# One core of Trainium2, attention with a gated MLP: the groups of values' products moved behind the last dense products of a block of keys

## The chip, the cores and the metric

The kernel runs on one core of a Trainium2 chip. The metric is the device time of one execution in microseconds (us). Six engines matter here: TensorE (PE in the profile, with its weight loads as PEld), VectorE (DVE), ScalarE (ACT), GpSimd (POOL), and SyncE (SP), which issues the DMAs in this kernel. Each engine works through its own list of instructions in order, and semaphores hold an instruction until what it needs is done. Products are summed in PSUM, which has eight banks of 128 x 512 numbers of 32 bits.

## What is computed

S = 2048 positions of width 512, one batch. `x` goes through an attention of 32 heads of width 16 that looks back over 255 positions and itself, and through an MLP of width 1792 with GELU; a gate of one number per position mixes the two. Cut to what matters:

```python
qkv = (x @ wqkv).reshape(B, S, 3, H, Dh)...      # H = 32, Dh = 16
scores = einsum("bhqd,bhkd->bhqk", q, k) * Dh ** -0.5
mask = (i - j >= 0) & (i - j < 256)
p = softmax(where(mask, scores, -1e9))
a = einsum("bhqk,bhkd->bhqd", p, v)... @ wo
b = gelu(x @ w1 + b1) @ w2 + b2
g = sigmoid((x * gate_w).sum(-1, keepdims=True))
out = g * a + (1 - g) * b
```

## The kernel before, in words

**Dense products.** Every dense product of 512 columns is made of three (lines 108 to 110), since each operand is split into a leading part and a rest. `dense()` (L913) is one long generator of these triples: the projections of four pieces of 512 positions, then eight turns of the MLP (`mlp`, L767), then the output projection (`final`, L857). A turn takes one piece and one half of the 1792 hidden columns. First comes its stage "u", seven hidden tiles of four triples each, with a GELU of six steps on ScalarE and VectorE behind each (`gelu`, L715); then its stage "y", 28 triples into four outputs. `fill(ns)` (L926) takes triples from the generator until a time has been filled up.

**Attention in units.** The heads are worked in 8 groups of four (g), the keys in 16 blocks of 128 (kb): 128 units u. The main loop (L943) goes over u; the maxima run LEAD = 12 units ahead of the rest. A unit has four parts i = 0 to 3. Each part has one score product for a row maximum (`att_max`, L519, tile `sm`, maximum taken by VectorE at L524) and one transposed score product (`att_exp`, L564, tile `st`, exponential by ScalarE at L586 into a tile `pt`), and then a quarter of a unit's dense work. The parts go in pairs, except in stage "u", where each goes alone: with m, s and f for the three, a unit is "m s m s f f m s m s f f" outside stage "u" and "m s f m s f m s f m s f" in it. A quarter is shorter than a triple, so now and then an f brings nothing. POOL cuts the edges of the exponentials to the window (L580).

**The values' products.** `att_pvs(u)` (L592) does nothing unless u is the last of four blocks, which are one piece of 512 positions. Then it makes one group: up to six blocks of keys, four heads, two halves, as small products that use 64 x 32 tiles of the array (L608), 2,880 in 32 groups. They sum into two tiles, `pv_sm` and `pv_st`. ScalarE copies one out (L629) and VectorE adds the other (L632); the sum is stored to DRAM (L636), and later divided (`att_norm`, L642).

**PSUM.** The dense products have two banks (tag d), the score products for the maxima three (tag sm), those for the exponentials three (tag st). A group takes one bank of tag sm and one of tag st until L629 and L632 have read them.

**What sets the order.** The order on each engine is the order in which the program writes instructions. A virtual clock places all that is not on TensorE: `after(ns, fn)` puts a step in a list of due times, and `tick(ns)`, called behind each product with its nominal length, writes the steps that have come due. `need(...)` writes steps early if something written now depends on them. `att_pvs` ticks for six pairs of blocks.

**Where the group stood.** In the unit u behind the four blocks (u divisible by 4), part i = PVAT = 2, behind its `st` product, for u up to 116 (lines 961 and 962). For the later u the group came at the unit's end (lines 969 and 970), and the last one inside the output projection (L983). Behind line 970 the unit's end also has the loads that SP issues for the next piece: keys (`load_ks`, L472) and values (`att_load_v`, L505, into the half of `vbuf` that the group just made was the last to read).

Of the kernel before, what the change touches and what calls it, by code (L numbers as in the profile page):

```python
# [32 lines left out]
def gated_mix(ctx: ExitStack, tc: tile.TileContext, x, wqkv, wo, w1, b1, w2, b2, gate_w, out):  # L33
# [81 lines left out]
    def after(ns, fn, *args):  # L115
        now[1] += 1
        heapq.heappush(todo, (now[0] + ns, now[1], fn, args))
# [7 lines left out]
    def tick(ns):  # L125
        now[0] += ns
        while todo and todo[0][0] <= now[0]:
            step_todo()

    def need(*keys):  # L130
        for key in keys:
            while key not in done:
                step_todo()
# [326 lines left out]
    def load_ks(g_, c):  # L460


        ready(c, g_, 1)
        n = 2 * NB
        put_pairs([f32(ks[64 * s + 4:64 * s + 52, slot(g_, c)]) for s in range(2)], SK[c], g_)
# [16 lines left out]
    def load_kd(g_, c):  # L482
        for t in range(max(c - 1, 0), c + 1):
            ready(t, g_, 1)
            k0 = 0 if t == c else T - W
            at = W if t == c else 0
            src = heads(SK[t], g_)[:, :, :, :, k0:].rearrange("s d u a c -> (s d u) a c")
            nc.sync.dma_start(f32(kd[0:96, slot(g_, c), :, at:at + T - k0]), src)

    def load_qd(g_, c):  # L490
        ready(c, g_, 0)
        put_pairs([f32(qd[48 * s:48 * s + 48, slot(g_, c)]) for s in range(2)], SQ[c], g_)

    def load_qs(g_, c):
        ready(c, g_, 0)
        need(("v", NT - 2, NB - 1))
        for s in range(2):
            v = f32(qs[64 * s + 4:64 * s + 52, :, c * T:(c + 1) * T])
            nc.sync.dma_start(v, part(SQ[c], g_, s).rearrange("r (a c) -> r a c", a=2))

    def att_load_v(g_, c):
        need(*[("v", c, b) for b in range(NB)])
        vt = vbuf[:, c % 2]
        dst = vt[:, 0:NB * 68].rearrange("p (j c) -> p j c", c=34)
        nc.sync.dma_start(dst, SV[c].rearrange("p j s c -> p (j s) c")[:, :, 34 * g_:34 * g_ + 34])  # L505
        vts[g_, c] = vt

    def att_max(g_, b, i):

        if b % RB == 0 and (g_, b // RB) not in Ms:  # L510
            Ms[g_, b // RB] = sb.tile([128, 2 * RB, 2], F32, tag="M", bufs=2, name=f"M{g_}_{b}")
        M = Ms[g_, b // RB]
        hb, pr = divmod(i, 2)
        c, n = b // NB, slot(g_, b // NB)
        j = 2 * (b % NB) + hb
        w = min(64 * (2 * b + hb + 1), W + 64)
        k1 = 64 * (j + 1) + W
        p = ps.tile([128, 320], F32, tag="sm", bufs=3, name=f"sm{g_}_{b}_{i}")
        nc.tensor.matmul(p[:, :w], qd[0:96, n, pr, 128 * j:128 * (j + 1)], kd[0:96, n, pr, k1 - w:k1],  # L519
                         start=True, stop=True)  # L520
        junk = cs.tile([128, 320], BF16, tag="jm", bufs=1, name=f"jm{g_}_{b}_{i}")

        def red():
            nc.vector.tensor_tensor_reduce(junk[:, :w], p[:, :w], mask[:, 320 - w:320], 1.0, -3e38,  # L524
                                           ALU.add, ALU.max, M[:, 2 * (b % RB) + hb, pr:pr + 1])
            done.add(("max", g_, b, i))
        tick(w / 2.4 + 13)
        after(100, red)
# [63 lines left out]
    def att_pvs(u):  # L592

        g_, kb = divmod(u, NKB)
        c, k = divmod(kb, NB)
        if k < NB - 1:
            return
        blocks = list(range(max(kb - 5, 0), kb + 1))
        pairs = list(zip(blocks, reversed(blocks) if c else blocks))
        n = g_ * NT + c - 1  # L600
        if n >= 0:
            need(("nd", *divmod(n, NT)))
        pv = [ps.tile([128, T], F32, tag=tag, bufs=3, name=f"pv{g_}_{c}_{tag}") for tag in ("st", "sm")]

        def mm(b, i, hf, q, e, rhs, start, stop):
            r = 64 * (1 ^ hf ^ i % 2)
            v = 68 * (b % NB) + 17 * (i % 2 * 2 + i // 2)
            nc.tensor.matmul(pv[r // 64][32 * i:32 * i + 32, q - c * T:e - c * T],  # L608
                             vts[g_, b // NB][r:r + 64, v:v + 32], rhs(r),
                             start=start, stop=stop, skip_group_check=True, tile_position=(r, 32 * i))  # L610
        if c == 0:
            for i in range(4):
                mm(0, i, 1, 0, 64, lambda r: nil[r:r + 64].broadcast_to([64, 64]), True, False)
        for j, pair in enumerate(pairs):
            for hf, b in enumerate(pair):
                need(("pt", g_, b, hf))
            ends = []
            for i in range(4):
                for hf, b in enumerate(pair):
                    k0 = b * 128 + hf * 64  # L620
                    q, e = max(k0, c * T), min(k0 + W + 64, S, (c + 1) * T)
                    mm(b, i, hf, q, e, lambda r: pts[g_, b][r:r + 64, hf, i // 2, q - k0:e - k0],
                       j == 0 and not (c == 0 and hf == 1), j == len(pairs) - 1)
                    ends.append(e - q)
            tick(max(ends) * 1.6 + 40)
        nd = sb.tile([128, T], F32, tag="tmp", bufs=3, name=f"nd{g_}_{c}")

        def half():
            nc.scalar.activation(nd, pv[0], AF.Copy)  # L629

        def ev():
            nc.vector.tensor_add(nd, nd, pv[1])  # L632
            after(HOLD if g_ * NT + c < NQ - 4 else 800, store)

        def store():
            nc.sync.dma_start(ND[c][g_ // 2][g_ % 2], nd)  # L636
            done.add(("nd", g_, c))
            if g_ % 2 == 1:
                after(NORM if g_ * NT + c < NQ - 4 else 3500, att_norm, c, g_ // 2)
        after(100, half), after(700, ev)  # L640
# [285 lines left out]
    def fill(ns):  # L926

        owed[0] += ns
        while owed[0] > 0:
            c = next(run)  # L930
            if c is None:
                owed[0] = -1e9
            else:
                owed[0] -= c
                tick(c)

    NU = NG * NKB
# [5 lines left out]
    for u in range(-LEAD, NU):  # L943
        m = u + LEAD
        gm, bm = divmod(m, NKB)
        step = STEP if u >= 0 else STEP0
        for i in range(4):
            if i == 1 and m % NB == 0 and NB <= m < NU - NB:
                load_kd(*divmod(m // NB + 1, NT)), load_qd(*divmod(m // NB + 1, NT))
            if i % 2 == 0:  # L950
                pair = (i, i + 1) if stage[0] != "u" else (i,)
            elif len(pair) == 2:
                continue
            else:
                pair = (i,)
            for op, i in [(op, k) for k in pair for op in ORDER[:3]] + [("f", k) for k in pair]:
                if op == "s" and u >= 0:
                    att_exp(u // NKB, u % NKB, i)
                if op == "m" and m < NU:
                    att_max(gm, bm, i ^ XOR)  # L960
                if op == "p" and i == PVAT and 1 <= u <= NU - LEAD:
                    att_pvs(u - 1)
                if op == "f":
                    fill(step / 4)
        if m < NU and bm % RB == RB - 1:
            after(900, att_rows, gm, bm // RB)
        if m % NB == QAT % NB and QAT <= m < QAT + NKB:
            load_qs(0, (m - QAT) // NB)
        if u > NU - LEAD:
            att_pvs(u - 1)  # L970
        if u % NB == 0 and NB <= u < NU - NB:
            load_ks(*divmod(u // NB + 1, NT))
        if u % NB == 2 and NB < u < NU - 3 * NB:
            load_qs(*divmod(u // NB + 3, NT))
        if u % NB == 0 and u >= 0:
            att_load_v(*divmod(u // NB, NT))
        if u - NU + NKB == YAT:
            for k in range(6):
                after(1500 + YGAP * k, load_y, *divmod(k, 2))
# [17 lines left out]
LEAD = 12  # L997
# [18 lines left out]
MXAT = 5500.0  # L1016
AHEAD = 9e3
STEP0 = 2750.0
PVAT = 2
HELD = 2  # L1020
YAT = 5
YGAP = 2500
# [21 lines left out]
```

## Time and profile before

| what | value |
|---|---|
| median of 3 runs | 750.57 us (749.57 to 752.2) |
| the profiled execution | 749.65 us |
| its span, first to last instruction | 747.9 us |
| granted TensorE clock | 1.00 |
| instructions | 17,961 |
| bytes read from and written to HBM | 108.53 MB, 62.39 MB |

Times below are in us from the start of the span unless a row says ns. In a row of a group the columns are: line, engine, operation, output<-inputs, shape, count | busy us, mean ns | idle time of the engine before it, with what ended it. In a row of the timeline: start, duration, engine, line, operation, shape, count, and in brackets the idle time ahead of it with what ended it. A TensorE row's duration is longer than the distance to the next row's start, since products overlap; the distance between two starts is what a product costs. A row of waits has the sum, the number of cases and the longest. A row of a window has, behind the stretch and its length, the busy time and count of each engine, then the granted clock, the share of the DMA engines and GB/s.

### The profile page before, as it was taken

How to read it: one execution, taken by the hardware profiler on the slowest of the kernel's cores; microseconds unless marked ns; L12 is line 12 of the kernel's file. 1: busy time of each engine (PE TensorE's matmuls, PEld its weight loads, DVE VectorE, ACT ScalarE, POOL GpSimd, SP SyncE). 2: the span in 40 equal slices, each digit the busy share in tenths (PEclk: the TensorE clock that was granted, in tenths of full speed). 3: DMA queues.
4: the chain of work that ended last, by engine and by line, in shares of the span. 5: the costliest groups of instructions: out<-in, count | busy, mean ns of one | idle time of the engine just before them, and what ended most of it. 6: DMA issues, size and time to landing. Idle time of an engine off the chain costs nothing.

```text
span 747.9 us, 17961 instructions
## 1 busy us (share of the span) xinstructions
PE 732.7 (98%) x6129; PEld 604.4 (81%) x6129; DVE 520.1 (70%) x1567; ACT 421.5 (56%) x972; POOL 372.3 (50%) x846
## 2 busy tenths in 40 slices
PE   8999999998999999999999999999999999999998
PEld 7888888876788888888887877888888888867786
DVE  4532325799768867986798689768867986784552
ACT  4434532358537845864695478438745863794550
POOL 4200000339756865876577568747765875630000
PEclk9999999999999999999999999999999999999999
DMA  9889798998895687899575979996799799468572
GB/s 326 319 272 404 261 391 273 291 293 182 270 259 134 162 243 205 175 222 271 146 179 149 242 211 234 249 237 152 178 256 235 194 224 270 136 181 226 191 252 111
DMA packets 179260, 172.12 MB, mean 230 GB/s; under 512 B 56673, under 2 KB 122977, under 8 KB 179169
## 3 DMA queue, kind: packets, MB, share of 16 engines
q1 hardware_dynamic: 179168, 170.97, 81.4%
q8 instruction: 49, 0.80, 0.5%
q14 instruction: 43, 0.34, 0.1%
HBM read 108.53 MB, written 62.39 MB: 229 GB/s over the span
## 4 chain that ended last, share of the span: by engine, by line
PE 85%; DVE 5%; ACT 3%; issue 3%; DMA 2%; SPq 1%; POOL 1%; DVEq 0%; ACTq 0%
PE sm L519 9%; PE st L564 8%; PE pv_sm L608 7%; PE y L108 7%; PE y L109 6%; PE y L110 6%; PE u L108 5%; PE u L109 5%; PE u L110 5%; PE qk L110 4%; PE qk L108 4%; PE qk L109 4%; PE a L108 2%; DVE jm L524 2%; PE v L108 2%
## 5 line engine op out<-in xcount | busy, mean ns | idle before, releaser
L524 DVE CUSTOM_DVE_ANT_0 jm<-sm,mask 128x320 bf16<-128x320 f32 (+4 forms) x512 | 238.1, 465 | 95.3 <-PE sm L519 61.1
L580 POOL TENSOR_SCALAR_AFFINE_SELECT pt<-pt 64x256 f32<-64x256 f32 (+1 forms) x538 | 227.7, 443 | 108.5 <-ACT pt L586 98.1
L586 ACT ACTIVATE pt<-st 128x320 f32<-128x320 f32 (+4 forms) x512 | 199.6, 424 | 139.1 <-PE st L564 136.0
L519 PE MATMUL sm<-kd,qd 96*128 96x320 f32 (+4 forms) x512 | 153.9, 312 | 6.3 <-DVE M L524 5.5
L564 PE MATMUL st<-qs,ks 128*128 128x320 f32 (+4 forms) x512 | 153.9, 309 | 1.9 <-ACT pt L586 1.9
L546 POOL CAST qs<-tt 4x256 fp32r<-4x256 f32 x256 | 124.6, 487 | 53.3 <-DVE tt L539 42.7
L519 PEld LDWEIGHTS sm<-kd,qd 96*128 96x128 f32 x512 | 96.3, 188 | 33.2 <-DVE M L524 13.7
L564 PEld LDWEIGHTS st<-qs,ks 128*128 128x128 f32 x512 | 97.1, 190 | 18.8 <-ACT pt L586 3.2
L108 PE MATMUL y<-w,h 128*128 128x512 f32 x224 | 88.5, 395 | 0.0
L109 PE MATMUL y<-w,h 128*128 128x512 f32 x224 | 87.9, 393 | 0.0
L110 PE MATMUL y<-w,h 128*128 128x512 f32 x224 | 87.9, 392 | 0.0
L108 PE MATMUL u<-mx,w 128*128 128x512 f32 x196 | 80.0, 408 | 0.0
L109 PE MATMUL u<-mx,w 128*128 128x512 f32 x196 | 77.4, 395 | 0.0
L110 PE MATMUL u<-mx,w 128*128 128x512 f32 x196 | 77.1, 393 | 0.0
L608 PE MATMUL pv_sm<-pt,vbuf 64*32 64x320 f32 (+4 forms) x1408 | 73.6, 346 | 0.2
L608 PE MATMUL pv_st<-pt,vbuf 64*32 64x320 f32 (+4 forms) x1408 | 73.3, 346 | 0.0
L608 PEld LDWEIGHTS pv_sm<-pt,vbuf 64*32 64x32 f32 x1408 | 50.2, 106 | 20.2 <-issue 2.4
L325 DVE TENSOR_TENSOR qke<-qk,qke 128x512 fp32r<-128x512 f32 x32 | 22.0, 688 | 46.9 <-ACT qke L322 33.2
L322 ACT ACTIVATE qke<-qk 128x512 fp32r<-128x512 f32 x32 | 19.1, 597 | 56.2 <-PE qk L110 32.5
L110 PEld LDWEIGHTS y<-w,h 128*128 128x128 f32 x224 | 42.0, 188 | 9.8
L338 POOL MEMSET vx<- 128x32 f32 x16 | 2.4, 156 | 89.0 <-DMA SQ<-qke 44.5
L608 PEld LDWEIGHTS pv_st<-pt,vbuf 64*32 64x32 f32 x1408 | 46.1, 106 | 0.0
(148 smaller groups left out, 1332.7 us busy)
## 6 DMA issues: line engine op xcount, KB each, us to landing
kd<-SK SPq DMA_DIRECT2D x32, 384.0 KB
qs<-SQ SPq DMA_DIRECT2D x64, 192.0 KB
mx<-XT SPq DMA_DIRECT2D x24, 512.0 KB
SQ<-qke SPq DMA_DIRECT2D x16, 512.0 KB
SK<-qke SPq DMA_DIRECT2D x16, 512.0 KB
ND<-nd SPq DMA_DIRECT2D x32, 256.0 KB
raw_w<-in_B_w_dram SPq DMA_DIRECT2D x28, 256.0 KB
ks<-SK SPq DMA_DIRECT2D x32, 192.0 KB
```

Source lines behind the costliest of these rows:

```text
L108: nc.tensor.matmul(p, lh, rh, start=first, stop=False)
L109: nc.tensor.matmul(p, lh, rl, start=False, stop=False)
L110: nc.tensor.matmul(p, ll, rh, start=False, stop=last)
L322: nc.scalar.activation(e[:, h], p, AF.Copy)
L325: nc.vector.tensor_sub(e[:, 1 - h], p, f32(e[:, h]))
L519: nc.tensor.matmul(p[:, :w], qd[0:96, n, pr, 128 * j:128 * (j + 1)], kd[0:96, n, pr, k1 - w:k1], start=True, stop=True)
L524: nc.vector.tensor_tensor_reduce(junk[:, :w], p[:, :w], mask[:, 320 - w:320], 1.0, -3e38, ALU.add, ALU.max, M[:, 2 * (b % RB) + hb, pr:pr ...
L546: nc.gpsimd.tensor_copy(dst, src.unsqueeze(1).broadcast_to([4, 2, RB, 32]))
L564: nc.tensor.matmul(p[:, :w], ks[:, slot(g_, kb // NB), pr, at:at + 128], qs[:, pr, k0:k0 + w], start=True, stop=True)
L580: nc.gpsimd.affine_select(out=v, in_=v, pattern=[[0, v.shape[1]], [1 - 2 * e, 64]], compare_op=ALU.is_ge, fill=0.0, base=-e, channel_multi ...
L586: nc.scalar.activation(pt[:, hf, pr, :w], p[:, :w], AF.Exp, scale=SCALE)
L608: nc.tensor.matmul(pv[r // 64][32 * i:32 * i + 32, q - c * T:e - c * T], vts[g_, b // NB][r:r + 64, v:v + 32], rhs(r), start=start, stop=s ...
```

## The change

The branch that wrote the group at part PVAT goes, with the constant, and the condition at the unit's end is widened, so that every group but the last is written there.

```diff
                 if op == "m" and m < NU:
                     att_max(gm, bm, i ^ XOR)
-                if op == "p" and i == PVAT and 1 <= u <= NU - LEAD:
-                    att_pvs(u - 1)
                 if op == "f":
                     fill(step / 4)
         if m < NU and bm % RB == RB - 1:
             after(900, att_rows, gm, bm // RB)
         if m % NB == QAT % NB and QAT <= m < QAT + NKB:
             load_qs(0, (m - QAT) // NB)
-        if u > NU - LEAD:
+        if u >= 1:
             att_pvs(u - 1)
         if u % NB == 0 and NB <= u < NU - NB:
             load_ks(*divmod(u // NB + 1, NT))
...
-PVAT = 2
```

NU is 128, LEAD 12, NB 4. What moves on the engines is shown at one group, that of the second piece of the third four heads (about 332 us into the span), in a stage "y". On TensorE, where the group begins, before (names: `sm_4_3` is block 4, part 3 of a maximum's product; `y_01` an output of the MLP; `pv_1` the group):

```order
L519 MATMUL sm_4_3_4555<-kd,qd 128x320
L564 MATMUL st_8_2_4558<-qs,ks 128x320
L608 MATMUL pv_1_sm<-pt_2_4129,vbuf 32x64
L608 MATMUL pv_1_st<-pt_7_4473,vbuf 32x64
L608 MATMUL pv_1_st<-pt_2_4129,vbuf 32x64
```

and now:

```order
L519 MATMUL sm_4_3_4555<-kd,qd 128x320
L564 MATMUL st_8_2_4558<-qs,ks 128x320
L519 MATMUL sm_4_2_4561<-kd,qd 128x320
L564 MATMUL st_8_3_4565<-qs,ks 128x320
L108 MATMUL y_00_4404<-w_6_2109,h_6_4402 128x512
L109 MATMUL y_00_4404<-w_6_2109,h_6_4402 128x512
L110 MATMUL y_00_4404<-w_6_2109,h_6_4402 128x512
L108 MATMUL y_01_4511<-w_3_1884,h_3_4142 128x512
L109 MATMUL y_01_4511<-w_3_1884,h_3_4142 128x512
L110 MATMUL y_01_4511<-w_3_1884,h_3_4142 128x512
L608 MATMUL pv_1_sm<-pt_2_4127,vbuf 32x64
L608 MATMUL pv_1_st<-pt_7_4473,vbuf 32x64
```

The unit's last pair of score products and two triples have moved ahead of the group. On TensorE, where the same group ends, before:

```order
L608 MATMUL pv_1_sm<-pt_2_4129,vbuf 32x128
L519 MATMUL sm_4_2_4617<-kd,qd 128x320
L564 MATMUL st_8_3_4622<-qs,ks 128x320
L108 MATMUL y_00_4404<-w_6_2119,h_6_4402 128x512
L109 MATMUL y_00_4404<-w_6_2119,h_6_4402 128x512
```

and now:

```order
L608 MATMUL pv_1_sm<-pt_2_4127,vbuf 32x128
L519 MATMUL sm_5_1_4643<-kd,qd 128x320
L564 MATMUL st_9_0_4648<-qs,ks 128x320
L519 MATMUL sm_5_0_4652<-kd,qd 128x320
L564 MATMUL st_9_1_4656<-qs,ks 128x320
L108 MATMUL y_01_4511<-w_4_1931,h_4_4213 128x512
L109 MATMUL y_01_4511<-w_4_1931,h_4_4213 128x512
```

Two pairs of the next block follow the group, where one pair and dense products did. On VectorE, around the addition that empties the group's second buffer (L632), before (`jm_4_2` is a maximum, the row behind it reads the result out, L812 ends an output of the MLP):

```order
L524 ISA jm_4_2_4619,M_4_4528<-sm_4_2_4617,mask 128x320
L524 ISA M_4_4528 128x1
L632 TENSOR_TENSOR nd_1_4616<-nd_1_4616,pv_1_sm 128x512
L812 SCALAR_TENSOR_TENSOR yo_00_4638<-y_00_4404,ya_00_1658 128x512
L524 ISA jm_5_1_4647,M_4_4528<-sm_5_1_4645,mask 128x320
```

and now:

```order
L524 ISA jm_4_2_4563,M_4_4524<-sm_4_2_4561,mask 128x320
L524 ISA M_4_4524 128x1
L812 SCALAR_TENSOR_TENSOR yo_00_4580<-y_00_4404,ya_00_1658 128x512
L524 ISA jm_5_1_4645,M_4_4524<-sm_5_1_4643,mask 128x320
L524 ISA M_4_4524 128x1
L524 ISA jm_5_0_4654,M_4_4524<-sm_5_0_4652,mask 128x320
L524 ISA M_4_4524 128x1
L632 TENSOR_TENSOR nd_1_4638<-nd_1_4638,pv_1_sm 128x512
L524 ISA jm_5_3_4671,M_4_4524<-sm_5_3_4669,mask 128x320
```

Two maxima of the next block stand ahead of the addition, where one maximum of the old block stood.

## The prediction

> **What bounds the kernel now.** The page comes first: its line of busy time, its chain of waits, and its costliest groups.
>
> ```profile
> span 747.9 us, 17961 instructions
> PE 732.7 (98%) x6129; PEld 604.4 (81%) x6129; DVE 520.1 (70%) x1567; ACT 421.5 (56%) x972; POOL 372.3 (50%) x846
> PE 85%; DVE 5%; ACT 3%; issue 3%; DMA 2%; SPq 1%; POOL 1%; DVEq 0%; ACTq 0%
> PE sm L519 9%; PE st L564 8%; PE pv_sm L608 7%; PE y L108 7%; PE y L109 6%; PE y L110 6%; PE u L108 5%; PE u L109 5%; PE u L110 5%; PE qk L110 4%; PE qk L108 4%; PE qk L109 4%; PE a L108 2%; DVE jm L524 2%; PE v L108 2%
> ```
>
> TensorE is the engine that sets the end: 85% of the chain, and all but 15.2 us (747.9 - 732.7) of the span. Its work is the same before and after. So the change can pay or cost in two ways only: what TensorE loses where one kind of product follows another, and what it waits for at the places that move. The view of waits on TensorE tells how much waiting there is at all.
>
> ```profile
> PE sm L519 <- DVE M L524: 5.5, 11, 1.0
> PE pv_st L608 <- ACT pt L586: 0.7, 1, 0.7
> PEld sm L519 <- DVE M L524: 13.7, 27, 1.2
> PEld st L564 <- ACT pt L586: 3.2, 6, 1.5
> PEld pv_st L608 <- ACT pt L586: 1.4, 2, 0.9
> ```
>
> The largest sum is a score product whose buffer VectorE has not read yet (L524): 13.7 us in 27 cases, counted on the weight loads, which see a wait longer than the products do. Values' products (L608) wait twice in 32 groups. So the trace holds some 18 us of such waiting (13.7 + 3.2 + 1.4), and little of it at the groups themselves.
>
> **What moves.** A group comes once in four blocks of keys, 32 in all; the branch that goes took blocks 1 to 116, so 29 of them move and three (blocks 120, 124 and the last) stay. Here is one as it is, from the timeline of TensorE: the last scores ahead, the group's first product, its last, and what follows (columns: start, duration, what).
>
> ```profile
> 332.16 0.31 PE L519 MATMUL sm<-kd,qd 96*128 96x320 f32 x1
> 332.31 0.31 PE L564 MATMUL st<-qs,ks 128*128 128x320 f32 x1
> 332.55 0.24 PE L608 MATMUL pv_sm<-pt,vbuf 64*32 64x64 f32 x1
> ...
> 334.75 0.27 PE L608 MATMUL pv_sm<-pt,vbuf 64*32 64x128 f32 x1
> 334.95 0.41 PE L519 MATMUL sm<-kd,qd 96*128 96x320 f32 x1
> 335.21 0.31 PE L564 MATMUL st<-qs,ks 128*128 128x320 f32 x1
> 335.36 0.39 PE L108 MATMUL y<-w,h 128*128 128x512 f32 x1
> 335.59 0.40 PE L109 MATMUL y<-w,h 128*128 128x512 f32 x1
> ```
>
> The group takes 2.40 us (332.55 to 334.95). What moves ahead of it is one pair of scores (0.15 + 0.15 us from start to start) and two dense triples (six products 0.23 apart, 1.39 us). So it starts about 1.7 us later; in a hidden stage ("u") it is one triple, one pair, one triple, which is the same 1.7 us. No instruction is added or taken away on TensorE.
>
> **Edge of the group, in.** After a score product the group starts 0.24 us later where 0.15 is usual (332.31 to 332.55): 0.09 lost. After a dense product, which is what the change makes of all 29, there are rows too, since the last groups already stand so.
>
> ```profile
> 686.54 0.40 PE L109 MATMUL y<-w,h 128*128 128x512 f32 x1
> 686.77 0.40 PE L110 MATMUL y<-w,h 128*128 128x512 f32 x1
> 687.10 0.24 PE L608 MATMUL pv_sm<-pt,vbuf 64*32 64x64 f32 x1
> ```
>
> 0.33 us where 0.23 is usual: 0.10 lost. The difference is 0.01 us, 29 times: 0 to +0.3 us, and I take +0.1.
>
> **Edge of the group, out.** To a score product: 0.20 (334.75 to 334.95), and then 0.26 instead of 0.15 (334.95 to 335.21). To a dense one, in a stage "u":
>
> ```profile
> 183.37 0.27 PE L608 MATMUL pv_st<-pt,vbuf 64*32 64x128 f32 x1
> 183.57 0.50 PE L108 MATMUL u<-xt,w 128*128 128x512 f32 x1
> 183.90 0.39 PE L109 MATMUL u<-xt,w 128*128 128x512 f32 x1
> ```
>
> Again 0.20, and then 0.33 instead of 0.23. Afterwards all 29 are followed by scores; by these rows that is worth 0.01 us each either way: -0.3 to +0.3 us, taken as 0. A page of the Trainium skill, "TensorEngine Tiling (Array Packing)", section "Key Properties", says that changing the tiling mode, not just the tile, drains TensorE. By that rule, the trace agrees: each change of shape costs something, about 0.1 us in and, by the rows above, some 0.2 us out. The rule alone would leave the sum as it is, since the count of changes, two per group, stays.
>
> **Waits at the group's entry.** Two of the 29 show one.
>
> ```profile
> 382.57 0.36 PE L564 MATMUL st<-qs,ks 128*128 128x320 f32 x1
> 383.60 0.30 PE L608 MATMUL pv_st<-nil,vbuf 64*32 64x64 f32 x2 [0.66 <-ACT pt L586]
> ...
> 654.89 0.30 PE L564 MATMUL st<-qs,ks 128*128 128x320 f32 x1
> 655.32 0.24 PE L608 MATMUL pv_st<-nil,vbuf 64*32 64x64 f32 x1
> ```
>
> 1.03 and 0.43 us where 0.24 is usual: 0.8 + 0.2 = 1.0 us of waiting for an exponential to leave its buffer. With at least one triple (0.70 us) between, most of it goes at the group. But the next score pair now stands there ahead of the group, and needs a buffer of the same three; in the first case ScalarE is a full us behind, so that pair can wait in the group's place. Bounds -1.0 to 0; I take -0.5, the middle, since one of the two ends is reached only if ScalarE catches up.
>
> **What stands behind the group.** Six score buffers are shared by products and group (three of a kind, the group holds one of each until its sums are read). Now both score pairs of the next block follow at once, or one pair and a triple, where one pair and dense work followed. VectorE has two maxima to take before it adds the group's halves, and till then the maxima's products turn in two buffers. From the same group, the row of ScalarE's half first and then VectorE:
>
> ```profile
> 335.08 0.60 ACT L629 ACTIVATE nd<-pv_st 128x512 f32<-128x512 f32 x1 [1.99 <-PE pv_sm L608]
> ...
> 335.41 0.49 DVE L524 CUSTOM_DVE_ANT_0 jm<-sm,mask 128x320 bf16<-128x320 f32 x1 [1.28 <-PE sm L519]
> 335.82 0.68 DVE L632 TENSOR_TENSOR nd<-nd,pv_sm 128x512 f32<-128x512 f32 x1
> 336.42 0.68 DVE L812 SCALAR_TENSOR_TENSOR yo<-y,ya 128x512 f32<-128x512 f32 x1
> 337.10 0.49 DVE L524 CUSTOM_DVE_ANT_0 jm<-sm,mask 128x320 bf16<-128x320 f32 x1
> ...
> 337.74 0.49 DVE L524 CUSTOM_DVE_ANT_0 jm<-sm,mask 128x320 bf16<-128x320 f32 x1
> ```
>
> Two maxima in a row start 0.64 us apart (337.10, 337.74). Put behind the same group, with its first score at 334.95: first maximum 335.41 to 335.90, second 336.05 to 336.54, then the add to about 337.2. The third score product comes at 334.95 + 0.26 + 3 x 0.15 + 1.39 = 337.05 and needs the first maximum: 1.1 us to spare. The fourth comes at 337.35 and needs the second: 0.8 us. In the groups where one triple stands there instead of two, 0.7 us less: 0.4 and 0.1 us. So nothing waits where VectorE has these alone. Where another addition (0.68) gets between, the fourth product can wait up to 0.6 us in those groups, five by the order. In the hidden stages VectorE is nearly full:
>
> ```profile
> 235.00:250.00 15.00, 15.00 (x103) 12.88 (x98) 13.92 (x45) 13.54 (x30) 12.22 (x26) 1.00 0.51 125
> ```
>
> 13.92 of 15 us, and still TensorE loses nothing there (15.00 of 15): a third score follows two triples and two pairs behind the group (about 2.0 us) and has room for one operation of 0.7 us ahead of its maximum (0.46 + 0.7 + 0.49 = 1.65), though not for two (2.35: 0.35 us of wait). By the order 13 groups are followed by stage "u". Bounds: 0, and 5 x 0.6 + 13 x 0.35 = +7.5 us if every one is hit. I take +0.4, near the lower end, because that row shows the engine as full as it gets and no wait. The fourth pair of the group's own block has lost its cover too, and follows the third as it does in the other three blocks of four. There 27 of 512 score products waited, 0.51 us each (13.7 / 27): 29 x 27 / 512 x 0.51 = 0.8 us. Bounds 0 and +0.8; I take +0.2, because the rest before the last group is only 1.7 us longer ago than it was.
>
> **The load of values.** It overwrites a half of vbuf that the group still reads, so SP's queue stops at it until the group's end. One such place, on SP, with the group's last product ahead of it:
>
> ```profile
> 368.51 0.27 PE L608 MATMUL pv_sm<-pt,vbuf 64*32 64x128 f32 x1
> ...
> 366.83 0.51 SPq L477 DMA_DIRECT2D ks<-SK  x1
> 368.91 0.54 SPq L505 DMA_DIRECT2D vbuf<-SV  x1
> 371.94 0.40 SPq L170 DMA_DIRECT2D raw_w<-in_B_w_dram  x1
> ```
> ```profile
> SPq L505 <- PE pv_sm L608: 6.6, 4, 2.1
> L178 ACT ACTIVATE w<-raw_w 128x512 fp32r<-128x512 f32 x28 | 17.7, 633 | 0.5 <-DMA raw_w<-in_B_w_dram 0.4
> ```
>
> Between 367.3 and 368.9 the queue stood still; now it stands 1.7 us longer wherever it gets there first. Behind the load wait stores of quotients and sums and, while weights come in, a raw_w load; their readers are ScalarE's copy (L178), then VectorE's subtraction. ScalarE waited for such a load for 0.4 us in the whole run, so there is little margin to see and no loss yet. In the place shown the queue is idle for 2.5 us after the load, which swallows 1.7. Bounds 0 and, with the three groups in the fourth turn losing all of it, +5; I take +0.2, near zero by that idle row.
>
> **The sum** is made against the profiled execution, 749.65 us (span 747.9 and 1.75 around it): +0.1 + 0 - 0.5 + 0.4 + 0.2 + 0.2 = +0.4, so 750.05. The median of the three runs shown is 750.57, 0.92 above that execution, so the forecast is 750.57 + 0.4 = **751.0 us**: no change. Changes below 0.3% (2.25 us here) cannot be told from none; the three runs themselves spread over 2.6 us.
>
> **Rivals.** *Faster:* scores right behind a group find VectorE with nothing left over, and the 13.7 us that weight loads of scores wait for L524 fall mostly in the block after and the block before a group. For it: the group gives VectorE over 1.2 us of rest (the 1.28 us ahead of 335.41). Against: that rest exists before too, only 1.7 us earlier. If a quarter of the waits goes: -3.4 and the -0.5 above, 750.57 - 3.9 = 746.7.
>
> *Slower, SP's queue:* the load of values holds raw_w in the fourth turn and the x loads at the turns' ends; ScalarE stops at L178 with exponentials behind it, and the scores wait for those. It decides once a load lands later than its copy stands in ScalarE's order, that is from about 0.4 us less margin than the trace shows. Two of three groups losing 1.7 us each: 750.57 + 3.4 = 754.0. Against: the 2.5 us of idle queue behind the load.
>
> *Slower, VectorE behind the group:* the two maxima ahead of the add, with an addition of the gelu between, in half the cases of the bound above: 7.5 / 2 = +3.8, so 754.3. Against: the full stretch at 235 us that loses nothing.
>
> *Slower, edges:* if a drain behind a 512-wide product were as much longer as the product (0.23 against 0.15), each of 29 entries would pay 0.08: +2.3, so 752.9. Against it is the row at 687.10, a measured 0.10. The rule on draining in the Trainium skill, "TensorEngine Tiling (Array Packing)", section "Key Properties", gives no length; a length that goes with the product would be this rival.
>
> *It does not do what it says:* the order of instructions shows 29 groups moved and all dense products ahead of them, so this one has no chance of its own.
>
> **How the numbers follow.** No change 0.54; faster 0.14; slower by SP 0.15, by VectorE 0.14, by the edges 0.03. That is faster 0.14, same 0.54, slower 0.32. The likeliest case alone spans 748.3 to 752.8 (0.3% to either side of the median). The range takes in most of both sides: 747.0 to 755.0, which leaves out most of the fastest case and the far end of the slow ones, some 2 in 10.
>
> **What would show it.** In the changed profile: products L608 still 0.33 us behind a dense start and scores 0.20 behind the group (edges right); no wait at the entries near 383 and 655 us (that term right), or a wait of a score pair there instead; VectorE's add (L632) ending some 0.6 us later behind each group, with no longer sum of sm waiting for M (that cover right, otherwise the third rival); the vbuf load issued right at the group's end in more of its 32 cases, with ScalarE's wait for raw_w still under 1 us (otherwise the second). The prediction is wrong if the waits of scores for VectorE, 13.7 us on the weight loads now, differ by more than about 3 us, or if TensorE's busy time differs while its instructions don't.

## The result, and the profile after

| | median | lowest to highest, runs |
|---|---|---|
| before | 750.74 us | 749.57 to 752.2, 6 |
| after | 755.42 us | 753.45 to 757.23, 6 |

The ratio is 1.0061, with a 95% interval of 1.0041 to 1.0082. The change makes the kernel slower by 4.7 us, where none was forecast, and the time lies above the range.

The page of the profiled execution of after (755.5 us), its lines of busy time and of the chain by engine:

```profile
span 753.8 us, 17980 instructions
PE 735.9 (98%) x6129; PEld 602.7 (80%) x6129; DVE 518.7 (69%) x1567; ACT 420.8 (56%) x972; POOL 371.7 (49%) x846
PE 85%; DVE 5%; DMA 3%; issue 3%; ACT 2%; SPq 1%; POOL 0%; DVEq 0%; ACTq 0%; POOLq 0%
```

TensorE makes the same 6,129 products and is busy 3.2 us longer. The span is 5.9 us longer; the view of waits shows what is added beside busy time:

```profile
PE sm L519 <- DVE M L524: 5.5, 9, 1.2
PEld sm L519 <- DVE M L524: 13.6, 28, 1.5
PE st L564 <- ACT nd L629: 2.6, 1, 2.6
PE st L564 <- DMA ks<-SK: 0.9, 1, 0.9
```

Scores wait for VectorE as before (13.6 us on the weight loads, 13.7 before). Two lines are new, each one single wait, and neither stands at a group that the change moved. In the timeline of TensorE:

```profile
683.04 0.39 PE L110 MATMUL y<-w,h 128*128 128x512 f32 x1
684.36 0.53 PE L564 MATMUL st<-qs,ks 128*128 128x320 f32 x2 [0.93 <-DMA ks<-SK]
...
691.07 0.40 PE L110 MATMUL y<-w,h 128*128 128x512 f32 x1
694.07 0.96 PE L564 MATMUL st<-qs,ks 128*128 128x320 f32 x2 [2.60 <-ACT nd L629]
694.83 0.63 PE L108 MATMUL y<-w,h 128*128 128x512 f32 x1
695.26 0.63 PE L109 MATMUL y<-w,h 128*128 128x512 f32 x1
```

Three losses follow one another: 1.1 us at 683 us (684.36 - 683.04 - 0.23), 2.8 at 691 (694.07 - 691.07 - 0.23), and then dense products stand 0.43 us apart instead of 0.23. That last one is the granted clock, in the windows of after:

```profile
690.00:695.00 5.00, 2.40 (x10) 1.74 (x9) 0.95 (x2) 1.51 (x4) 0.00 (x0) 0.84 0.38 121
695.00:700.00 5.00, 5.00 (x15) 3.94 (x14) 2.23 (x5) 1.69 (x5) 0.00 (x0) 0.50 0.70 220
```

The clock was 0.50 from 693.4 to 700.3 us. Setting the same dense product of both traces side by side, after is 1.08 us *ahead* at 681 us, 0.10 behind at 686, and 5.85 behind from 701 us to the end. So up to 681 us the 29 moved groups have cost TensorE nothing, and the next 20 us take 6.9: 1.1 and 2.8 of stops, and about 3.0 of half clock. No moved group lies within those 20 us; the last one, written at unit 116 (piece 0 of the last four heads), ended at 658.1, only 0.8 us later than before, since by then TensorE was 0.9 ahead.

What hangs on that group is the division of the last heads (`att_norm`), which is a chain: sums stored (ND, L636), denominators loaded (den, L646), inverted on VectorE (L650), stored (RD, L653), numerators and inverses loaded (num, rb, L658), multiplied (L662), stored (OT, L665), and loaded for the output projection (ot, L703). On VectorE, before and then after:

```profile
668.09 0.42 DVE L574 TENSOR_TENSOR pt<-pt,cut 128x256 f32<-128x256 f32 x1
668.43 0.34 DVE L650 RECIPROCAL den<-den 128x32 f32<-128x32 f32 x1
668.69 0.63 DVE L737 TENSOR_TENSOR h<-x1h,h 128x512 fp32r<-128x512 f32 x1
```

```profile
667.57 0.69 DVE L737 TENSOR_TENSOR h<-x1h,h 128x512 fp32r<-128x512 f32 x1
668.17 0.42 DVE L574 TENSOR_TENSOR pt<-pt,cut 128x256 f32<-128x256 f32 x1
669.53 0.69 DVE L731 SCALAR_TENSOR_TENSOR x1h<-sqh,x1h 128x512 f32<-128x512 f32 x1 [0.94 <-ACT sqh L728]
670.83 0.43 DVE L574 TENSOR_TENSOR pt<-pt,cut 128x256 f32<-128x256 f32 x1 [0.61 <-ACT pt L586]
671.17 0.68 DVE L725 SCALAR_TENSOR_TENSOR sqh<-sqh,x1h 128x512 f32<-128x512 f32 x1
671.78 0.34 DVE L650 RECIPROCAL den<-den 128x32 f32<-128x32 f32 x1
```

The steps of the division are due so many ns behind the group's store. With the group later, the reciprocal is written five rows later in VectorE's list, behind two rows that wait for ScalarE: 3.35 us later, though the engine itself is 1.1 us ahead. On SP, before and then after (start, duration of the issue, what):

```profile
660.05 0.34 SPq L636 DMA_DIRECT2D ND<-nd  x1
...
668.80 0.34 SPq L653 DMA_DIRECT2D RD<-den  x1
...
672.32 0.41 SPq L480 DMA_DIRECT2D ks<-SK  x1
...
677.08 0.34 SPq L636 DMA_DIRECT2D ND<-nd  x1
...
681.49 0.61 SPq L646 DMA_DIRECT2D den<-ND  x1
682.22 0.37 SPq L665 DMA_DIRECT2D OT<-num  x1
682.64 1.40 SPq L703 DMA_DIRECT2D ot<-OT  x3
...
684.55 0.43 SPq L703 DMA_DIRECT2D ot<-OT  x1
```

```profile
661.51 0.34 SPq L636 DMA_DIRECT2D ND<-nd  x1
...
672.15 0.34 SPq L653 DMA_DIRECT2D RD<-den  x1
...
674.85 0.42 SPq L480 DMA_DIRECT2D ks<-SK  x1
...
677.77 3.88 SPq L636 DMA_DIRECT2D ND<-nd  x1
...
685.11 0.61 SPq L646 DMA_DIRECT2D den<-ND  x1
685.76 1.41 SPq L703 DMA_DIRECT2D ot<-OT  x3
...
688.03 0.37 SPq L665 DMA_DIRECT2D OT<-num  x1
...
693.33 0.32 SPq L703 DMA_DIRECT2D ot<-OT  x1
```

The lateness grows from step to step: 1.5 us at the group's own ND, 3.35 at RD. SP stands at RD until 672.15, so nine transfers (RD to vbuf) are issued in a crowd. The keys (ks) in it go out 2.5 us later than before; a load of keys is what the stop at 683 us waits for. The next group's ND takes 3.88 us to issue, and its den comes 3.6 us later. And the store OT, which stood ahead of the three ot loads, now stands behind them: it is issued 5.8 us later. The fourth ot load waits for it to land and goes out 5.3 us after it, and holds SP's list meanwhile (before, it went out 2.3 us after OT, right behind the ya load, so it hardly waited). The buffer of `num` is what `nd` of piece 2's group needs next, which is the stop at 691 us; on ScalarE, after:

```profile
693.42 0.60 ACT L629 ACTIVATE nd<-pv_st 128x512 f32<-128x512 f32 x1 [6.19 <-DMA OT<-num]
```

### The profile page after: what moved, and what is told of

It reads as the page before. It is cut to its first block, busy times and chain, and to the rows that moved or that the text cites. A ratio compares the mean times of both kernels' runs of the same rounds, so it can differ in the third digit from the quotient of the medians.

```text
span 753.8 us, 17980 instructions
## 1 busy us (share of the span) xinstructions
PE 735.9 (98%) x6129; PEld 602.7 (80%) x6129; DVE 518.7 (69%) x1567; ACT 420.8 (56%) x972; POOL 371.7 (49%) x846
## 4 chain that ended last, share of the span: by engine, by line
PE 85%; DVE 5%; DMA 3%; issue 3%; ACT 2%; SPq 1%; POOL 0%; DVEq 0%; ACTq 0%; POOLq 0%
PE sm L519 10%; PE st L564 8%; PE pv_sm L608 7%; PE y L108 6%; PE y L109 6%; PE y L110 6%; PE u L108 6%; PE u L109 6%; PE u L110 5%; PE qk L110 4%; PE qk L108 4%; PE qk L109 4%; PE a L108 2%; PE v L108 2%; PE v L110 2%
## 5 line engine op out<-in xcount | busy, mean ns | idle before, releaser
L524 DVE CUSTOM_DVE_ANT_0 jm<-sm,mask 128x320 bf16<-128x320 f32 (+4 forms) x512 | 237.9, 465 | 103.1 <-PE sm L519 65.5
L586 ACT ACTIVATE pt<-st 128x320 f32<-128x320 f32 (+4 forms) x512 | 197.5, 424 | 125.0 <-PE st L564 121.2
L519 PEld LDWEIGHTS sm<-kd,qd 96*128 96x128 f32 x512 | 96.4, 188 | 34.7 <-DVE M L524 13.6
L108 PE MATMUL y<-w,h 128*128 128x512 f32 x224 | 89.5, 399 | 0.0
L109 PE MATMUL y<-w,h 128*128 128x512 f32 x224 | 88.8, 397 | 0.0
L110 PE MATMUL y<-w,h 128*128 128x512 f32 x224 | 88.7, 396 | 0.0
L629 ACT ACTIVATE nd<-pv_st 128x512 f32<-128x512 f32 x32 | 19.1, 597 | 63.0 <-PE pv_sm L608 51.6
```

The source lines that it names most:

```text
L108: nc.tensor.matmul(p, lh, rh, start=first, stop=False)
L109: nc.tensor.matmul(p, lh, rl, start=False, stop=False)
L110: nc.tensor.matmul(p, ll, rh, start=False, stop=last)
L586: nc.scalar.activation(pt[:, hf, pr, :w], p[:, :w], AF.Exp, scale=SCALE)
```

## The experiments

Two things had to be told apart: which groups make the loss, and through what. Theory A: it is the one group at unit 116 ("block 116's"). Its rival B: it is the other 28. Theory C, formed after the first four runs: the lateness of that group goes into the two lists, through the reciprocal above all. Its rival D: a group that ends 1.7 us later costs by itself. The table has, for each run but e11, when the reciprocal started, when the store OT and the fourth ot load were issued, and how long the next group's ND took to issue, in the profiled execution; the stops of TensorE behind 675 us of 0.5 us or more that the kernel before does not have; and the median. The stops are distances between starts less the usual one. "Before" ran with each, at medians of 750.57 to 750.81.

| run | L650 | OT | fourth ot | ND takes | stops, us (at) | median | ratio, 95% |
|---|---|---|---|---|---|---|---|
| before | 668.43 | 682.22 | 684.55 | 0.34 | | 750.74 | |
| after | 671.78 | 688.03 | 693.33 | 3.88 | 1.1 (683), 2.8 (691) | 755.42 | 1.0041 to 1.0082 |
| e1 | 667.01 | 680.84 | 683.42 | 0.58 | | 749.24 | 0.9976 to 0.9994 |
| e2 | 672.63 | 688.00 | 693.59 | 3.90 | 3.1 (691), 1.7 (720) | 756.8 | 1.0066 to 1.0094 |
| e3 | 671.12 | 687.93 | 692.58 | 4.69 | 1.2 (682), 1.1 (695), 3.5 (717) | 756.65 | 1.0075 to 1.0106 |
| e4 | 671.40 | 685.47 | 688.02 | 3.30 | 1.1 (683), 3.4 (716) | 755.01 | 1.0051 to 1.0083 |
| e5 | 667.08 | 683.53 | 687.77 | 0.76 | 1.3 (715) | 751.26 | 0.9986 to 1.0036 |
| e6 | 672.01 | 684.25 | 688.98 | 1.00 | 0.9 (708), 3.3 (717) | 755.93 | 1.0041 to 1.009 |
| e7 | 671.94 | 686.58 | 689.29 | 4.31 | 1.3 (683), 0.5 (695), 2.2 (718) | 753.77 | 1.0022 to 1.0062 |
| e8 | 671.95 | 685.64 | 691.30 | 1.26 | 1.7 (690), 2.8 (718) | 754.09 | 1.0028 to 1.0063 |
| e9 | 667.04 | 680.81 | 683.45 | 0.34 | | 749.77 | 0.998 to 1.0008 |
| e10 | 667.84 | 681.74 | 684.27 | 0.34 | 0.5 (716) | 748.68 | 0.9956 to 0.998 |

**e1, that group back at its old place; 28 stay moved.**

```diff
+                if op == "p" and i == PVAT and u == NU - LEAD:
+                    att_pvs(u - 1)
...
-        if u >= 1:
+        if u >= 1 and u != NU - LEAD:
             att_pvs(u - 1)
```

> 28 of the 29 moved groups stay behind their block's dense products; the group of block 116 alone goes back amid its scores. Theory A (the loss is made in the last 65 us, by one group that moves while the groups of blocks 120 and 124 stay): no wait of ScalarE's copy L629 for the store OT<-num, clock 1.00 throughout, 749.5 us (748.5 to 751). Theory B (every moved group costs about 0.16 us, by VectorE or SP behind it): 28/29 of the loss stays, 755 us (754 to 756).

749.24 us: the loss is gone, and the kernel is faster than before by 1.5 parts in a thousand. In its view of waits three of TensorE's have shrunk: `pv_st` for `pt` (0.7 us) and `sm` for `nd` (0.4) are gone, `sm` for M fell from 5.5 to 4.9; at 681 us TensorE is 1.5 us ahead of before.

**e2, only that group moved.**

```diff
+                if op == "p" and i == PVAT and 1 <= u < NU - LEAD:
+                    att_pvs(u - 1)
...
-        if u >= 1:
+        if u >= NU - LEAD:
             att_pvs(u - 1)
```

> Only the group of block 116 moves; the other 28 stay amid their scores. Theory A: the whole loss, 756 us (754.5 to 758), with the wait of L629 for OT<-num of some 6 us and a stretch at half the clock. Theory B: 1/29 of the loss, 751 us (750 to 752).

756.8 us: the one group alone makes the whole loss. Theory A stands, B falls.

**e3, the stop at 691 us taken away by another buffer** for `nd` of piece 2's group, so that it need not wait for OT.

```diff
-        nd = sb.tile([128, T], F32, tag="tmp", bufs=3, name=f"nd{g_}_{c}")
+        nd = sb.tile([128, T], F32, tag=("tmp", "raw")[u == 123], bufs=3 - (u == 123), name=f"nd{g_}_{c}")
```

> The changed kernel, where the sum of the group of block 124 goes to an idle buffer of another kind, so that ScalarE's copy L629 need not wait until the quotient of an earlier group has been stored; no instruction moves. Theory A: the stop of 2.8 us at 691 us and the half clock behind it (about 2 us) go, the wait of 1.1 us for the load of keys at 683 us stays: 750.7 us (749.5 to 752). Theory B: 755.4 us (754.5 to 756.5).

A miss: that stop goes, yet 756.65 us. The wait has only moved to the output projection. Its timelines of TensorE and VectorE:

```profile
717.31 0.39 PE L110 MATMUL a<-wo,ot 128*128 128x512 f32 x1
721.07 0.50 PE L108 MATMUL a<-wo,ot 128*128 128x512 f32 x1 [3.37 <-DVE ao L879]
```

```profile
712.30 0.75 DVE L879 SCALAR_TENSOR_TENSOR ao<-a,g,ao 128x512 f32<-128x512 f32 x1
718.26 0.35 DVE L650 RECIPROCAL den<-den 128x32 f32<-128x32 f32 x1 [5.21 <-DMA den<-ND]
718.53 0.63 DVE L662 TENSOR_TENSOR num<-num,rb 128x512 f32<-128x512 f32 x1
719.08 1.28 DVE L709 TENSOR_TENSOR ot<-ot 128x512 fp32r<-128x512 f32 x2
720.27 0.74 DVE L879 SCALAR_TENSOR_TENSOR ao<-a,g,ao 128x512 f32<-128x512 f32 x1
```

VectorE stands 5.21 us at the reciprocal of piece 3, the last one, whose denominators come late, and L879, which empties the PSUM bank that the next block of outputs needs, stands behind it. All stops of the table from 715 us on lie at this same product. So a buffer was only the first place where the lateness showed.

**e4, product and store OT due sooner**, for this division alone, so that OT stands ahead of the ot loads again.

```diff
-        for ns, fn in zip(DIVS[c == NC - 1], (rcp, keep, back, mul, store)):
+        for ns, fn in zip(DIVS[2 if (t, c) == (0, NC - 1) else c == NC - 1], (rcp, keep, back, mul, store)):
...
-DIVS = ((8000, 10000, 16000, 23000, 25000), (4500, 5700, 8500, 17000, 18500))
+DIVS = ((8000, 10000, 16000, 23000, 25000), (4500, 5700, 8500, 17000, 18500),
+        (4500, 5700, 8500, 15300, 16000))
```

> The changed kernel, where the store of that quotient (OT<-num) is due 2.5 us sooner on the program's clock, and so stands ahead of three loads ot<-OT in SP's list, as before the change. Theory A: the store goes out some 2 us sooner than 688.0 us, the copy L629 waits that much less, TensorE's stop shrinks from 2.8 to about 0.8 us and may stay short enough to keep the clock: 752 us (750.5 to 754). Theory B: 755.4 us (754.5 to 756.5).

A miss: 755.01 us. OT stands ahead of the ot loads, but both stand behind the next den, which is late as ever (684.76), and the reciprocal is late as ever.

**e5, the reciprocal due sooner**, and nothing else. The first line of e4's diff, and as the third entry:

```diff
+        (3000, 5700, 8500, 17000, 18500))
```

> The changed kernel, but the reciprocal L650 of piece 0's last two heads is due 1.5 us sooner, which puts that one row of VectorE's list ahead of L737, L574, L731 and L725, where it stood before the change; no other row of any engine moves. Theory C (the late reciprocal holds SP's list at the store RD<-den, nine transfers are then issued in a bunch, the store ND<-nd of the next group needs 3.9 us to be issued in place of 0.3, and every division behind it is some 3.5 us late): the reciprocal starts at about 667.6 us in place of 671.78, the store ND<-nd of the next group takes under 0.7 us, its den load is issued at about 681.5 in place of 685.11, the stops at 683 and 691 us and any of 3 us behind them are gone, and the time is 749.5 to 750.5 us. Rival D (the group itself ends 1.7 us later, and that alone hands the lateness down): the den load of the next group stays behind 684 us and the time is 754 to 756 us.

751.26 us, 4.2 less than after; ND takes 0.76 us, the next den is issued at 680.16. The mechanism is right; the size is not all of it. Its 12 runs go from 748.03 to 757.75, and OT still stands behind the three ot loads. The four runs above 753 us are those with a mean granted clock of 0.992 to 0.995, the other eight had 0.999 or more: whether the clock falls behind the stops that are left makes most of the spread.

**e6, three loads of 512 KB taken out of the crowd.**

```diff
-                after(1500 + YGAP * k, load_y, *divmod(k, 2))
+                after(1500 + YGAP * k + (0, 0, 0, 14500, 19000, 17000)[k], load_y, *divmod(k, 2))
```

> The changed kernel with the reciprocal as late as the change made it, but three loads of 512 KB (one qd<-YB, two kd<-YB) are taken out of the bunch behind RD<-den and issued 14.5 to 19 us later. Theory C with the bunch as its link: the reciprocal stays near 671.8 us, yet the store ND<-nd of the next group takes under 0.7 us, its den load is issued at 680 to 682 us, and the time is 750 to 752 us. If the late reciprocal reaches the end by its own chain (num, rb, product, store OT, load ot) and the bunch is only beside it: den is early again, but a stop of 3 us stays at the first group of the output projection or at 691 us, and the time is 754 to 756 us.

755.93 us, and no verdict on the crowd: ND takes 1.00 us and den is early (681.30), but the two kd loads now stand at 699.3 us ahead of piece 1's ot loads, which needed 2.54 us to issue, and held OT and ND of the later pieces. The crowd was moved, not removed.

**e7, the faster kernel e1 with the reciprocal made late**, where the change put it. To e1, the first line of e4's diff, and as the third entry:

```diff
+        (6000, 7200, 10000, 17000, 18500))
```

> The fast version (28 groups moved, block 116's at its old place), with the reciprocal of piece 0's last two heads due 1.5 us later, which puts that one row of VectorE's list behind L737, L574, L731 and L725, where the change put it; no other row of any engine moves. Theory C: the reciprocal starts at about 671.4 us in place of 667.01, the store ND<-nd of the next group takes 2 us or more in place of 0.58, the den load of the next group is issued behind 683 us in place of 680.13, and the time is 753 to 756 us, though the group's own products are as early as before the change. Rival D: 749.2 us as without the edit.

The store RD and the loads behind it are due as much later, but beside e1 the reciprocal is the only row of VectorE, ScalarE, GpSimd and SP that changes its place. 753.77 us, 4.5 more than e1, with the group itself as early as ever. One row of VectorE's list is worth as much as e5 gave back (4.2). Theory C holds: the group need not be late for most of the loss. That a late group costs something as well is left for e10.

**e8, the three loads cut to a quarter of their partitions**, their places kept; the kernel leaves out three quarters of what they bring.

```diff
-        nc.sync.dma_start(v, YB[t].rearrange("(i j p) f -> i p j f", j=2, p=128)[i])
+        p0 = 96 if 2 * t + i > 2 else 0
+        nc.sync.dma_start(v[p0:], YB[t].rearrange("(i j p) f -> i p j f", j=2, p=128)[i, p0:])
```

> The changed kernel, but the three loads of 512 KB behind RD<-den (one qd<-YB, two kd<-YB) carry only 32 of 128 partitions, 128 KB each, so three quarters of two pieces' MLP result are not loaded; their places in SP's list stay, and so does every row of the other engines. The earlier try that moved them only moved the crowd: it then stood ahead of the ot loads. Theory C with the crowd as its link: the reciprocal stays at about 671.8 us, the store ND<-nd of the next group takes under 0.7 us, its den load is issued at 680 to 682 us, no stop of 3 us is left, and the time is 750 to 752 us. If the lateness goes down the reciprocal's own chain (RD, rb, product, OT, ot): the den load is early again, but a stop of 2 to 3.5 us stays at 691 us or in the output projection, and the time is 753.5 to 755.5 us.

754.09 us: the second of its two cases. ND takes 1.26 us in place of 3.88, yet OT is issued at 685.64, behind the ot loads, and `nd` waits for it to land. So the bytes of the crowd are not needed for most of the loss: it makes one of two paths late, and the other is late without it.

**e9, the same loads cut in the faster kernel e1.**

> The control for the run before it: the fast version (28 groups moved) with the same three loads cut to 32 partitions, so that it too does not load three quarters of two pieces' MLP result. Where the loads cost the fast version nothing: 748.5 to 749.5 us. Where they cost it time of their own, it is below 748, and the run before must be read against this one.

749.77 us, a little above its range (e1: 749.24; the intervals overlap): the loads cost that kernel nothing that shows, and e8 can be read as it stands.

**e10, reciprocal, product and store all due sooner; all 29 groups stay moved.** The first line of e4's diff, and:

```diff
+        (3000, 5700, 8500, 15300, 16000))
```

> The changed kernel with both late steps of piece 0's last division due sooner, the reciprocal by 1.5 us and product and store OT<-num by 1.7 and 2.5 us, so that the reciprocal, the product and the store stand in VectorE's and SP's lists where they stand in the fast version; the group of block 116 stays behind the last dense products, as the change put it. Theory C (these two orders carry the whole loss): 749 to 750 us, as the fast version, with runs closer together than the 748.0 to 757.8 us of the run with the reciprocal alone. Rival D (a group that ends 1.7 us later costs by itself): 751 us or more.

748.68 us, 748.06 to 749.8 in 8 runs, 0.3 below its range. D falls: the late group costs nothing once the rows that hang on it stand where they stood. Its SP rows, to be set beside the two lists above:

```profile
668.21 0.34 SPq L653 DMA_DIRECT2D RD<-den  x1
...
676.48 0.34 SPq L636 DMA_DIRECT2D ND<-nd  x1
...
681.03 0.61 SPq L646 DMA_DIRECT2D den<-ND  x1
681.74 0.39 SPq L665 DMA_DIRECT2D OT<-num  x1
```

It is the fastest kernel here, with e1 next; their intervals overlap (0.9956 to 0.998, 0.9976 to 0.9994), so which of them is better stays open.

**e11, those due times in the kernel before.** The lines of e10, without the change.

> The kernel before the change, with the due times of the run that moved all groups and made both late steps sooner. Here no group stands later, so the reciprocal and the store only move ahead of where they already stood in time. If the gain of that run (0.9968) came from the moved groups, this one stays at 750 to 751.5 us; if it came from an earlier division alone, this one is at 748.5 to 749.5 us as well.

750.82 us beside 750.81, ratio 0.9999 (0.9987 to 1.0011), 11 runs. An earlier division gains nothing by itself, so what e10 gains over before comes with the moved groups. The control is not quite clean: here the fourth ot load also moved one place up in SP's list, ahead of the ya load, the two steps that split what it brought (L706, L709) moved too, and in the trace TensorE stops for 1.3 us at 716 us, where before does not.

## Why the prediction was wrong, step by step

*Edges.* Right in size. In the group shown, the last dense product starts at 335.38 in after and the group's first at 335.71:

```profile
335.38 0.40 PE L110 MATMUL y<-w,h 128*128 128x512 f32 x1
335.71 0.24 PE L608 MATMUL pv_sm<-pt,vbuf 64*32 64x64 f32 x1
```

That is 0.33 us, as forecast. Of the 29 moved groups 27 enter so, 0.32 or 0.33 us behind a dense product; two (at 368.8 and 639.8 us) still follow a score, at 0.24, so "all 29" was not exact, at no cost. All 29 are left after 0.20 us. The loss does not go with the width of the product ahead, and the rival on edges falls.

*Waits at the entry.* Right: both are gone; near the first of them a score now stops for 0.38 us in the group's place. That was feared, but of a score that waits for an exponential; this one waits for a maximum of VectorE (L524).

*Behind the group.* Right in kind, and it costs nothing: VectorE's add ends 2.1 us behind the group in place of 1.5, and the sum of waits of scores for VectorE is the same (13.6 us). So neither the rival on VectorE nor the faster one, which had these waits shrink, came to pass.

*The load of values.* ScalarE's wait for raw_w rose from 0.4 us to 2.5 in three cases:

```profile
ACT w L178 <- DMA raw_w<-in_B_w_dram: 2.5, 3, 0.8
```

That is more than the 1 us named as the sign of the rival on SP's queue, but TensorE was 1.1 us ahead at 681 us, and e1, the faster kernel, has more of it (3.4 us in five cases). So that rival fell too, though it was near: it looked at the right queue and at the wrong load.

*The sum* is where it fails. Its first step said that the change "can pay or cost in two ways only": at the borders between kinds of products, and in waits "at the places that move". The waits that cost came some 25 us and more behind the last moved group. The sum asked what each group does to TensorE, to the buffers of the scores and to one load, took the 29 groups as alike, and left out what hangs on a group's sums: of L636 and `att_norm` it has no term. For 28 of them no such term was needed: e1, where they moved, is at 749.24 beside 750.57. Even there the sum was off, -1.3 measured in place of about +0.4, but that is small beside what was left out. For the group at unit 116 one was: only some 40 us lie between its end and the first product of the output projection (657.3 to 697.9 us before), and the division's steps share the lists of VectorE and SP with everything else. The group's own 0.8 us became 1.5 at ND, 3.35 at the reciprocal and 5.8 at OT. The missing term measured 6.2 us (755.42 against 749.24, by e1) or 6.7 (against 748.68, by e10), half clock included. The time came out on the slower side, which had a chance of 0.32, but for none of the causes priced there. One sign that the prediction gave for being wrong did come: TensorE's busy time differs, 735.9 us in place of 732.7, with the same products; the half clock makes them longer.

It could have been read ahead. The order shows, on VectorE and SP, that the reciprocal and the store fall behind other rows. The trace of before shows what these rows cost: behind the reciprocal come two waits for ScalarE, 0.94 and 0.61 us in the trace of after, and as much in that of before. And in SP's view of waits before the change, RD already waits for the reciprocal, and the longest case, 3.9 us, is this very one, ahead of 668.80, so a later reciprocal had no slack there:

```profile
SPq L653 <- DVE den L650: 7.7, 6, 3.9
```

*What is shown, and what is not.* Shown: the one group makes the loss (e1, e2); the reciprocal's place makes most of it (e5, e7), and reciprocal, product and store together all of it (e5, e10). The 691 us stop and the half clock are where it came out, not its cause (e3; the profiled executions of e2 and e3 kept the full clock and took 755.31 and 754.12 us). The clock adds to the size: about 3.0 us in the trace of after. Not shown: how much the crowd behind RD adds, since e6 was confounded and e8 has the store late anyway; and where e10 gains its 2 us over before, since its profiled execution was the slowest of its 8 (749.8) and its span (748.0) is no shorter. In that trace the same three waits have shrunk as in e1, and TensorE is 0.6 us ahead of before at 681 us, but it loses that again at the product at 716 us.

## What to carry to other kernels

When a block of work moves, follow its result to the last reader, not only the block: in engines that work in order, a step that is written later stands behind other rows and takes on their waits too, so that 0.8 us can become 5.8. Look for the one copy of a repeated step that lies near the end or feeds a serial chain, and cost it by itself; the order of each engine ahead of the run, set beside the waits of the rows that it falls behind, shows it. When a stop is taken away and the time stays, look for the same lateness at the next place where it can show, and mend the earliest step in the chain.

## What the runs showed of the hardware

The granted clock fell to 0.50 at some stops and not at others of the same length: TensorE was idle 2.6 us and the clock was halved for 6.8 us (after); 2.7, 3.2 and 3.3 us idle led to 3.4 us at half clock (e8, e6, e4); 3.4 us idle in e3 and 2.9 in e2 led to none. So in these traces a stop of about 3 us cost between nothing and 3.0 us more than its own length. The Trainium skill, "TensorE: Matmul & The Clock Gate", section "What's actually happening", has a free-running window of about 3.4 us: the lengths at half clock agree with one and two of these. By the section "HAM oscillation — how this bites in real kernels" of the same page of the Trainium skill, gaps above about 3.4 us are the ones to avoid; here 2.6 us were enough once, and 3.4 were not.

A store that took 0.34 us to issue took 3.3 to 4.7 us where some 2 MB of transfers had been issued in the 6 us before it (after, e2, e3, e4, e7), and a load of what had just been stored was issued 5.3 us behind the store where 1 MB of loads had gone out just ahead of the store (after), 4.4 us of it waiting, and 2.3 us behind it where none had (before).
